# The 48 weight loads issued by GpSimd instead of SyncE

## The chip, the cores and the metric

One core of one Trainium2 chip runs one program. The metric is device time in microseconds (us) of one execution; lower is better. The profile comes from one further execution of the same program.

## The reference, cut to what matters

The inputs q, k, v are 4 x 8 x 576 x 64 in float32, omega is 128 x 64 and the weights of two feed-forward blocks are **float64** in memory. Three parts follow each other:

```python
phi(x):  h = x*scale @ omega.T - sum((x*scale)**2)/2;  h -= max(h, last axis);  exp(h)/sqrt(128)
kv = einsum('bhsm,bhsd->bhmd', phi(k), v);  z = sum(phi(k), axis=2)
x  = (phi(q) @ kv) / (phi(q) . z + 1e-6)           # then to [2304, 512]
h  = x @ w_in;  y = max(0.01*h, h) @ w_out         # w_in 512x2048, w_out 2048x512
h  = y @ w2_in; s = h*softmax(h); s = layernorm(s)*g_ln;  out = s @ w2_out   # 512x1024, 1024x512
```

## The kernel before, in words

The tokens are cut into 18 tiles of 128. For each tile there is a k unit and a q unit (load, squares, scale, transpose, projection on TensorE, maximum on VectorE, exp on ScalarE); the k units add up kv on TensorE, the q units draw x from it. The first block runs over pairs of tiles j = 0 to 8: stage 1 (`st1`, h = x @ w_in, L1087 for j = 0 in float32, L1093 for the rest as three float16 products), its evacuation (L1109 to L1111), stage 2 (`st2`, L1133 for j = 0, L1137 for the rest). The second block (`mlp2_in`, L1255 and L1373; `mlp2_out`, L1578) follows.

**The weights.** All four matrices come in 48 pieces of 128 rows by 512 float64 values, so 128 x 4096 bytes or 512 KB each: 16 of w_in and 16 of w_out early in the run (loads 0 to 31 in order of issue), 8 of w2_in and 8 of w2_out late (loads 32 to 47). `piece` (L363) does one. It takes one of four staging buffers `wraw`, starts the load (L374), and has the float64 bits turned into float32: either ScalarE reads the buffer (L388) or GpSimd does (L393, after which VectorE joins the sign, L396), and in both cases VectorE reads it last (L399) and the buffer is free. So load n + 4 cannot start before the L399 of load n has ended.

**What sets the order.** A planner in the program (`Issue`) plays all work through once, with durations written into the code, and writes every instruction down at the moment it is planned. Each engine then runs its own instructions strictly in that written order, each one waiting for its semaphores. Loads, stores and DMA transposes are planned on one queue, "DMA", and written into SyncE's stream: 113 copies and 119 transposes. An engine that issues a DMA waits for what the DMA needs (a free buffer, say) at its place in the stream, and what is written behind waits with it. GpSimd issues no DMA before the change; it computes some squares (L675), the first step of 26 weight pieces (L393), high parts of features (L876) and two steps of some weight cuts (L338, L340).

TensorE too has a fixed order. Up to 300 small products with zeros (L488, `warm_up`) are planned into places where it has nothing else; they are instructions like the others and take their time.

**The written order around the loads.** Loads and GpSimd's own instructions follow each other so: loads 0, 1, 2; L675 of the first k tile pair; L393 of load 0; load 3; L393 of load 1; loads 4 to 11; L675 of the first q pair; load 12; L393 of load 11; load 13; L393 of load 12; loads 14 to 20; L393 of load 18; load 21; L393 of load 21; loads 22, 23, 24; L393 of load 23; load 25; two L876; L338 and L340; load 26; L876; load 27; L876; L338; load 28; L340; L393 of load 28; loads 29, 30, 31; the last two L393 of this group. Late in the run: loads 32, 33, 34; L393 of load 32; load 35; L393 of loads 33, 34, 35; load 36; its L393; loads 37, 38; L393 of load 37; load 39; and so on in turn.

In SyncE's own order the load of the first k pair (L244, raw<-in_k_dram) and the two of omega (L499) stand among loads 0 to 3, and the first big transpose T<-hl (L705) stands between loads 21 and 22.

Of the kernel before, what the change touches and what calls it, by code (L numbers as in the profile page):

```python
# [27 lines left out]
class Issue:  # L28
# [13 lines left out]
    SP = {"DMA": (0.42, 2.3), "DT": (1.27, 1.65)}  # L42
# [121 lines left out]
def either(key, n, a, b):  # L164

    return a() if n in X[key] else b()
# [14 lines left out]
def linear_attention_moe_kernel(  # L181
# [14 lines left out]
    V, A, G, PE, SP = nc.vector, nc.scalar, nc.gpsimd, nc.tensor, nc.sync  # L196
# [74 lines left out]
    def mk(pool, tag, shape, dt):  # L271
        return pool.tile(shape, dt, name=tag, tag=tag, bufs=BUFS[tag])
# [90 lines left out]
    def piece(src, r0, c0, n, x, pool, nr):  # L363

        yield "get", "wraw"
        u = h = None
        if src.dtype == F32:
            yield "op", "DMA", 1.58, lambda: SP.dma_start(out=x, in_=src[r0:r0 + 128, c0:c0 + n])
        else:
            h = {}  # L370

            def load():
                h["r"] = mk(pool, "wraw", [128, n, 2], I32)
                SP.dma_start(out=h["r"].rearrange("p n w -> p (n w)"),  # L374
                             in_=src[r0:r0 + 128, c0:c0 + n].bitcast(I32))
            yield "op", "DMA", 1.58, load

            hw = lambda: h["r"][:, :, 1].bitcast(F32)  # L380
            xi = x.bitcast(I32)

            def shift():
                yield "op", "V2", 0.38, lambda: V.tensor_scalar(out=xi, in0=xi, scalar1=3, scalar2=None,
                                                               op0=ALU.logical_shift_left)

            def sign_A():
                yield "op", "A", 0.63, lambda: A.activation(out=x, in_=hw(), func=AF.Prelu, scale=2.0 ** -112,  # L388
                                                            alpha=-2.0 ** 32)
                yield from shift()  # L390

            def sign_V():
                yield "op", "G", 0.75, lambda: G.tensor_scalar(out=x, in0=hw(), scalar1=2.0 ** -112, scalar2=1.0,  # L393
                                                               op0=ALU.mult, op1=ALU.mult)
                yield from shift()
                yield "op", "V2", 0.62, lambda: V.scalar_tensor_tensor(  # L396
                    out=xi, in0=h["r"][:, :, 1], scalar=-(1 << 31), in1=xi, op0=ALU.bitwise_and, op1=ALU.bitwise_or)
            yield from either("ya", nr, sign_A, sign_V)
            yield "op", "V2", 0.62, lambda: V.scalar_tensor_tensor(  # L399
                out=xi, in0=h["r"][:, :, 0], scalar=29, in1=xi, op0=ALU.logical_shift_right, op1=ALU.bitwise_or)  # L400
        yield "put", "wraw"
# [1282 lines left out]
```

## Time and profile before

| | |
|---|---|
| time, median of 3 runs | 702.56 us (702.26, 702.56, 704.22) |
| the profiled execution, its time and its span | 701.82 us, 700.0 us |
| mean granted TensorE clock in it | 0.996 of full speed |
| busy share of the span: TensorE, VectorE, ScalarE, GpSimd | 98%, 70%, 59%, 20% |
| DMA queue of SyncE | 183536 packets, 80.37 MB, 49.8% of 16 engines' span |
| chain of work that ended last, largest shares | TensorE 74%, issue 7%, DMA 6%, ScalarE 6%, VectorE 4%, GpSimd 1% |

PE is TensorE, PEld its weight load, DVE VectorE, ACT ScalarE, POOL GpSimd, SP or SPq SyncE and its DMA queue. "Idle before, releaser" says how long the engine stood before an instruction and which work ended that; issuing a DMA does not count as busy. A time of a DMA "to landing" runs from its issue to the moment its semaphore shows all data there.

### The profile page before, as it was taken

The numbers are of one execution on the slowest core, as the hardware profiler recorded it, in microseconds if no ns is written. First come the engines' busy times: TensorE is split into PE (matmuls) and PEld (weight loads), VectorE is DVE, ScalarE is ACT, GpSimd is POOL, SyncE is SP. The second block draws the span as 40 slices with busy tenths as digits, with TensorE's granted clock in tenths as the row PEclk, the third lists the DMA queues.
The fourth block names the chain that finished last, engine by engine and source line by source line (L and its number), as shares of the span: only waits on it lengthen the run. The fifth ranks groups of instructions, "written<-read, shape, count | busy, mean of one in ns | idle before, by whom it ended". The sixth has DMA issues, their size and how long they took to land.

```text
span 700.0 us, 13443 instructions
## 1 busy us (share of the span) xinstructions
PE 684.4 (98%) x5120; PEld 453.4 (65%) x5120; DVE 486.6 (70%) x1211; ACT 416.1 (59%) x848; POOL 139.9 (20%) x174
## 2 busy tenths in 40 slices
PE   7989999999999999999999999999999999999997
PEld 7989885587766666767767666666654444444443
DVE  6988889699866567755965558953489897976410
ACT  4777987797766665656546535655244366756611
POOL 2010220433221110111101012534031111322210
PEclk9999999999999999999999999999999999999999
DMA  9895997696536442633725556501003323464541
GB/s 287 239 276 173 250 230 164 122 154 150 118 73 97 106 93 59 115 70 76 137 46 106 107 165 225 123 1 31 1 6 79 64 44 81 76 122 90 121 121 45
DMA packets 183600, 81.23 MB, mean 116 GB/s; under 512 B 146416, under 2 KB 175088, under 8 KB 183536
## 3 DMA queue, kind: packets, MB, share of 16 engines
q1 hardware_dynamic: 183536, 80.37, 49.8%
q8 instruction: 40, 0.66, 0.4%
q14 instruction: 24, 0.20, 0.1%
HBM read 41.75 MB, written 4.72 MB: 66 GB/s over the span
## 4 chain that ended last, share of the span: by engine, by line
PE 74%; issue 7%; DMA 6%; ACT 6%; DVE 4%; POOL 1%; SPq 1%; POOLq 0%; ACTq 0%; DVEq 0%
PE h L1093 18%; PE y L1137 16%; PE h L1578 13%; PE h L1373 6%; PE h L1087 3%; PE h L1255 3%; PE y L1373 3%; PE kv L853 2%; ACT qe L789 2%; PE y L1133 2%; DMA v<-in_v_dram 2%; PE a L1011 1%; DVE mx L774 1%; DMA raw<-in_k_dram 1%; DMA scr<-in_omega_dram 1%
## 5 line engine op out<-in xcount | busy, mean ns | idle before, releaser
L1137 PE MATMUL y<-w,g 128*128 128x512 f16 x768 | 176.0, 379 | 0.0
L1093 PEld LDWEIGHTS <-w 128*128 128x128 f16 x1536 | 148.2, 98 | 25.1 <-issue 1.1
L1137 PEld LDWEIGHTS <-g 128*128 128x128 f16 x768 | 73.9, 98 | 77.2 <-DVE g L1111 0.7
L1093 PE MATMUL h<-xy,w 128*128 128x256 f16 x960 | 111.9, 273 | 0.0
L1111 DVE TENSOR_TENSOR g<-h,g 128x512 f16<-128x512 f32 x64 | 44.0, 688 | 45.6 <-ACT g L1110 45.4
L1109 ACT ACTIVATE h<-h 128x512 f32<-128x512 f32 x64 | 38.1, 595 | 61.0 <-PE h L1093 60.6
L1093 PE MATMUL h<-xT,w 128*128 128x256 f16 x576 | 67.8, 273 | 0.1
L1578 PE MATMUL h<-wo,w 128*128 128x512 f16 x288 | 64.1, 379 | 0.0
L789 ACT ACTIVATE qe<-a,nb,sc 128x128 f32<-128x128 f32 x128 | 47.2, 468 | 15.6 <-DVE nb L780 13.8
L1578 PEld LDWEIGHTS <-w 128*128 128x128 f16 x288 | 28.2, 98 | 34.0
L774 DVE TENSOR_REDUCE mx<-a 128x4 f32<-128x512 f32 x63 | 41.5, 684 | 10.3 <-PE a L767 8.1
L876 POOL TENSOR_SCALAR qf<-qe 128x512 f16<-128x512 f32 x32 | 20.2, 634 | 110.5 <-ACT qe L789 84.6
L1110 ACT ACTIVATE g<-h 128x512 f16<-128x512 f32 x64 | 38.7, 604 | 1.2
L1588 ACT ACTIVATE osb<-h,c_out 128x512 f32<-128x512 f32 x18 | 12.3, 682 | 44.0 <-PE h L1578 41.1
L879 DVE SCALAR_TENSOR_TENSOR qf<-qe,qf 128x512 f16<-128x512 f32 x32 | 23.7, 740 | 16.1 <-POOL qf L876 16.1
L789 ACT ACTIVATE ke<-a,nb,sc 128x128 f32<-128x128 f32 x64 | 23.4, 469 | 16.6 <-DVE nb L780 15.0
L675 POOL TENSOR_TENSOR scr<-raw 128x1024 f32<-128x1024 f32 (+1 forms) x8 | 14.4, 1805 | 91.3 <-DMA raw<-in_q_dram 81.1
L1578 PE MATMUL h<-wo,lnT 128*128 128x512 f16 x144 | 32.2, 379 | 0.0
L1373 PE MATMUL h<-w 128*128 128x512 f16 x126 | 29.8, 379 | 0.7 <-ACT w L1431 0.7
L667 DVE TENSOR_REDUCE sq<-scr 128x16 f32<-128x1024 f32 (+1 forms) x20 | 22.1, 1107 | 11.5 <-POOL scr L675 7.6
L1373 PEld LDWEIGHTS <-w 128*128 128x128 f16 x168 | 16.4, 98 | 20.7 <-issue 1.0
L1087 PE MATMUL h<-xT,w 128*128 128x256 f32 x128 | 29.7, 383 | 0.0
(256 smaller groups left out, 1298.4 us busy)
## 6 DMA issues: line engine op xcount, KB each, us to landing
wraw<-in_moe_w_in_dram SPq DMA_DIRECT2D x24, 512.0 KB, 5.8
wraw<-in_moe_w_out_dram SPq DMA_DIRECT2D x24, 512.0 KB, 4.6
v<-in_v_dram SPq DMA_DIRECT2D x12, 512.0 KB, 4.4
raw<-in_k_dram SPq DMA_DIRECT2D x8, 512.0 KB, 4.2
raw<-in_q_dram SPq DMA_DIRECT2D x8, 512.0 KB, 4.8
out_dram<-osb SPq DMA_DIRECT2D x16, 256.0 KB, 2.3
v<-in_v_dram SPq DMA_DIRECT2D x6, 128.0 KB, 3.6
raw<-in_k_dram SPq DMA_DIRECT2D x4, 128.0 KB, 3.8
```

The costliest lines, as they stand in the source:

```text
L667: yield "op", "V", 0.07 + 0.54 * m, lambda: V.tensor_reduce(out=st["sq"], in_=tiles(st["scr"]), axis=AX.X, op=ALU.add)
L774: yield "op", "V", 0.6, lambda: V.tensor_reduce(out=u["mx"][:, hh::2], in_=w["ps"], axis=AX.X, op=ALU.max)
L789: A.activation(out=x[:, h, :], in_=w["ps"][:, h, :], func=AF.Exp, scale=st["sc"], bias=u["nb"][:, 2 * h + hh:2 * h + hh + 1])
L879: yield "op", "V" if stay else "V2", 0.62, lambda: V.scalar_tensor_tensor(out=w["f"][:, :, 1, :], in0=w["e"], scalar=2.0 ** 14, in1=w["f"] ...
L1087: PE.matmul(ps[:, f, :], lhsT=stash(w1, c * KC + kc)[:, o:o + 128], rhs=xT[j][:, kc, :], start=(kc == 0), stop=(kc == KC - 1))
L1093: PE.matmul(ps[:, f, :], lhsT=w1[:, c * KC + kc, w, o:o + 128], rhs=xT[j][:, :, xo + kc, :], start=(n == 0), stop=(n == 3 * KC - 1))
L1109: yield "op", "A", 0.48, lambda: A.activation(out=ps, in_=ps, func=AF.Prelu, scale=2.0 ** -19, alpha=0.01)
L1110: yield "op", "A", 0.48, lambda: A.activation(out=gg[:, 0], in_=ps, func=AF.Copy)
L1111: yield "op", "V", 0.6, lambda: V.tensor_tensor(out=gg[:, 1], in0=ps, in1=gg[:, 0], op=ALU.subtract)
L1137: PE.matmul(y_ps[j][t], lhsT=gg[:, a, f, ts], rhs=w2[:, 2 * p + f, w, :], start=(ends[0] and f == 0 and n == 0), stop=(ends[1] and f == 1 ...
L1373: PE.matmul(dst, lhsT=lhs(x, c), rhs=rhs(w, c), start=(fresh and n == c == 0), stop=(n == 2 and c == 1), skip_group_check=True)
L1578: PE.matmul(ps, lhsT=t[:, a, f, :], rhs=W["o"][:, f, w, :], start=(j == 0 and f == 0), stop=(j == 2 and f == KF2 - 1))
```

## The change: what it does

The engine that issues the load in `piece` is GpSimd (`G`) instead of SyncE (`SP`). The planner still plans the load on its "DMA" queue with the same duration, so the places in the written order stay as they are; only the stream into which the instruction goes is another one.

```diff
             def load():
                 h["r"] = mk(pool, "wraw", [128, n, 2], I32)
-                SP.dma_start(out=h["r"].rearrange("p n w -> p (n w)"),
+                G.dma_start(out=h["r"].rearrange("p n w -> p (n w)"),
                              in_=src[r0:r0 + 128, c0:c0 + n].bitcast(I32))
             yield "op", "DMA", 1.58, load
```

## Rows read from the trace of the kernel before

**Rows 1.** Stretches: window; us; PE, PEld, DVE, ACT, POOL busy (count); clock; DMA; GB/s.
```profile
0.00:20.00 20.00, 15.93 (x167) 14.94 (x167) 13.78 (x31) 9.69 (x19) 3.96 (x12) 1.00 0.93 298
...
40.00:60.00 20.00, 17.48 (x158) 16.71 (x155) 15.79 (x45) 14.13 (x34) 0.47 (x2) 0.91 0.87 251
60.00:80.00 20.00, 18.91 (x138) 17.31 (x137) 18.29 (x57) 17.28 (x42) 2.20 (x3) 1.00 0.70 210
80.00:100.00 20.00, 20.00 (x141) 17.46 (x140) 16.39 (x41) 16.85 (x36) 7.69 (x9) 1.00 0.93 213
...
400.00:450.00 50.00, 50.00 (x339) 33.06 (x338) 36.18 (x67) 25.09 (x54) 14.63 (x18) 1.00 0.61 176
```

**Rows 2.** Waits of TensorE: engine, line, releaser: us in total, times, longest.
```profile
PE kv L853 <- DMA v<-in_v_dram: 2.0, 2, 1.6
...
PE h L502 <- DMA scr<-in_omega_dram: 1.0, 1, 1.0
```

**Rows 3.** Waits of SyncE's own DMA queue, same columns.
```profile
SPq L374 <- DVE w L399: 33.1, 20, 5.0
```

**Rows 4.** Chain that ended last, in order of time: start us, us, what.
```profile
5.06 7.63 DMA scr<-in_omega_dram
...
68.47 7.50 DMA T<-hl
...
493.73 1.73 PE h L1255 x8
```

**Rows 5.** Timeline of TensorE: start us, us, engine, line, names, count.
```profile
7.66 4.14 PE L488 MATMUL kv<-nil 128*128 128x128 f16 x62
...
44.85 1.09 PE L735 MATMUL h<-ident,qe 128*128 128x128 f32 x8
```

**Rows 6.** Line 374: issue ns min/median/max, then landing us.
```profile
L374 SPq DMA_DIRECT2D wraw<-in_moe_w_in_dram x24: 327/386/1163, 1.2 to 421.4; - x24
...
DMA to landing us min/median/max: 3.4/5.4/8.6
```

**Rows 7.** GpSimd by line, 0 to 130 us: busy us, mean ns, idle before.
```profile
L340 POOL TENSOR_TENSOR w<-w 128x512 f16<-128x512 f32 x3 | 3.8, 1263 | 0.2
```

**Rows 8.** Timeline of ScalarE: start us, us, what, idle before and releaser.
```profile
9.28 0.69 ACT L388 ACTIVATE w<-wraw 128x512 f32<-128x512 f32 x1 [7.28 <-DMA wraw<-in_moe_w_in_dram]
...
16.91 0.68 ACT L388 ACTIVATE w<-wraw 128x512 f32<-128x512 f32 x1 [0.42 <-DMA wraw<-in_moe_w_in_dram]
...
42.24 0.67 ACT L388 ACTIVATE w<-wraw 128x512 f32<-128x512 f32 x1 [4.15 <-DMA wraw<-in_moe_w_out_dram]
42.82 1.13 ACT L789 ACTIVATE qe<-a,nb 128x128 f32<-128x128 f32 x4
```

**Rows 9.** Timeline of SyncE's DMA queue, same columns.
```profile
33.76 0.33 SPq L374 DMA_DIRECT2D wraw<-in_moe_w_in_dram  x1
34.36 0.33 SPq L374 DMA_DIRECT2D wraw<-in_moe_w_out_dram  x1
...
68.47 3.87 SPq L705 DMA_TRANSPOSE T<-hl  x1
72.45 1.46 SPq L374 DMA_DIRECT2D wraw<-in_moe_w_out_dram  x3
```

**Rows 10.** Timeline of GpSimd, same columns.
```profile
34.78 1.89 POOL L675 TENSOR_TENSOR scr<-raw 128x1024 f32<-128x1024 f32 x1 [26.32 <-DMA raw<-in_q_dram]
37.99 0.79 POOL L393 TENSOR_SCALAR w<-wraw 128x512 f32<-128x512 f32 x1 [1.31 <-DMA wraw<-in_moe_w_in_dram]
...
80.11 0.62 POOL L876 TENSOR_SCALAR qf<-qe 128x512 f16<-128x512 f32 x1 [0.45 <-ACT qe L789]
...
460.95 1.47 POOL L340 TENSOR_TENSOR wi<-wi 128x512 f16<-128x512 f32 x1
```

**Rows 11.** Timeline of VectorE, 69 to 73 us: the last readers of two buffers.
```profile
69.27 0.68 DVE L399 SCALAR_TENSOR_TENSOR w<-wraw,w 128x512 int32<-128x512 int32 x1
...
71.38 0.68 DVE L399 SCALAR_TENSOR_TENSOR w<-wraw,w 128x512 int32<-128x512 int32 x1
```

## The prediction

> **What bounds the kernel now.** I read the stretches first [rows 1]. TensorE is busy without a gap from 80 us on (20.00 of 20.00, and 50.00 of 50.00 between 400 and 450), so nothing that the loads gain there can shorten the run. Its idle time is at the front: 20 - 15.93 = 4.1 us in 0 to 20, 2.5 us in 40 to 60, 1.1 us in 60 to 80. DMA is crowded in just these stretches (shares of 0.93 and 0.87, about 300 GB/s). TensorE's own waits [rows 2] say what ends those gaps: 1.0 us for omega, 2.0 us for v. Beside them it runs a fixed filler, such as 62 products with zeros from 7.66 us for 4.14 us [rows 5], which no earlier load takes away. The chain of waits [rows 4] shows two DMAs on it that are slow for their size: omega's 32 KB needs 7.63 us, since it was issued behind three weight loads and more on the same queue, and T<-hl takes 7.50 us. Last I read the streams of ScalarE, SyncE and GpSimd [rows 8 to 10] and compared the written order with their times.
>
> So time can be won only out of some 3 us of DMA waits at the front; it is lost wherever an engine's fixed order makes TensorE wait for something later than today.
>
> **What the change removes.** SyncE issues 48 instructions fewer, 0.33 to 0.39 us each [rows 6], and no longer stands 33.1 us in 20 waits for a free staging buffer [rows 3]. I cost that at nothing: it was waiting with the load that came next in any case, its buffer's last reader L399 ended the wait, and what stands behind (raw, v, transposes) waits for readers of its own; if one of them was ready meanwhile, up to the longest such wait, 5.0 us, is a gain for that DMA, and TensorE's 3 us of DMA waits are all that can be won with it. The loads are bound by the four buffers, not by SyncE; only few can start sooner. The clear case is loads 22 to 24: their buffers come free at about 69.95, 71.4 and 72.06 (the first and the third are 69.27 + 0.68 and 71.38 + 0.68 [rows 11]), and SyncE issues them from 72.45 on, after T<-hl, whose issue alone takes 3.87 us [rows 9].
>
> **What it adds.** GpSimd must describe 48 transfers. The trace has no such instruction. Bounds: SyncE's 0.33 us [rows 6] from below, GpSimd's longest kind, L675 with 1.89 us [rows 10], from above. I take 1.26 us, the mean of L340 [rows 7], a whole GpSimd pass over 512 columns and near the middle. A description that costs less than nothing is excluded, since the engine must at least dispatch it. In throughput that is harmless: 48 x 1.26 = 60 us more on an engine that is idle 80% of the run. What counts is the order.
>
> **What moves, in order of time.**
>
> *A, start.* Loads 0 to 2 now run beside the first k load and omega instead of between them. A 512 KB load occupies the engines for 0.524 MB / 298 GB/s = 1.8 us [rows 1]. The first k load can be slowed by up to that, and I take half, 0.9; omega's wait of 1.0 us [rows 2] can go, for the zeros ahead of it in TensorE's order end at 7.66 + 4.14 = 11.80 [rows 5], 0.9 us before omega lands at 12.69 [rows 4]. Sum about 0; ends -1.0 and +0.8.
>
> *B, load 4.* ScalarE already waits 0.42 us for it at 16.91 [rows 8], and the next thing it does is on TensorE's path. GpSimd is free there, so the load is later by the description alone, 1.26 - 0.39 = 0.9 us at most; with some crowding gone I take +0.4; ends 0 and +0.9.
>
> *C, load 13.* This is the place where the order bites. On SyncE it went out at 34.36 [rows 9]. On GpSimd it stands behind L675, which waits for the first q pair until 34.78 and ends at 36.67, then behind load 12, then behind L393 of load 11, which ends at 37.99 + 0.79 = 38.78 [rows 10]. So it starts 4.4 us later and takes 1.26 us to describe: 40.04. From the end of issue to landing a load takes 3.4 - 0.4 = 3.0 us at least and 5.4 - 0.4 = 5.0 us in the median [rows 6]: it lands at 43.0 to 45.0. Today ScalarE stands 4.15 us before L388 of this very load, until 42.24, and the exp of the first q tile is next in its order at 42.82 [rows 8]; TensorE transposes that exp's result at 44.85 [rows 5]. So TensorE gets it 0.8 to 2.8 us later. I take the middle, +1.8. TensorE's waits for v of 2.0 us [rows 2] may shrink, but they would only become a wait at 44.85. If L675 and load 11 come sooner, nothing is lost: ends -2.0 (the v waits gone, load 13 in time) and +2.8.
>
> *E, T<-hl.* TensorE turns to this transpose's result as soon as it is there, at 68.47 + 7.50 = 75.97 [rows 4]. Loads 22 to 24 stood behind it; now load 22 can be described from 69.95, and its data flow some 3 us later, beside the last 3 us of T. At a third of the engines for the weights T loses +1.0; ends 0 (T was limited by its own issue, 3.87 us) and 5.3 (three loads of 1.8 us pass it whole).
>
> *F, 80 to 130 us.* Load 25 now stands ahead of L876, which ran at 80.11 [rows 10]; with a description of 1.26 us, and no longer a wait for its buffer than the one that SyncE had, L876 is 1.3 us later, and VectorE and a transpose wait for it. TensorE's gapless work hides it [rows 1]: 0, up to +1.3.
>
> *G, the late loads.* Load 35 goes from before the L393 of load 32 to behind it, so behind that load's landing, and the next ones follow. VectorE, 72% busy (36.18 of 50), will stand a few us. TensorE's f16 work is the cover, without a gap there [rows 1], and the last piece of w2_in is cut at 460.95 + 1.47 = 462.42 [rows 10], 31 us ahead of its first use at 493.73 [rows 4]: 0, up to +2 if an evacuation is caught behind a waiting VectorE.
>
> Sum: 0 + 0.4 + 1.8 + 1.0 + 0 + 0 = **+3.2 us** on the profiled 701.82, so 705.0. That execution lies 0.74 below the median of 702.56, with 1.8 us outside its span that the change leaves alone; on the median it is **705.8 us**.
>
> **The rivals.** *R1, relief, not slower.* The loads leave SyncE's queue, so omega and v no longer sit behind them: 1.0 + 2.0 us of TensorE's waits go [rows 2]. The point that decides is load 13: if it lands by 42.2, C's loss is nothing. For it: omega's 7.63 us and a crowded queue. Against it: L675 waits for a q load on GpSimd itself. Time 702.6 - 3.0 = 699.6.
>
> *R2, nothing.* The same 16 DMA engines, four buffers, a TensorE order that hides the rest; C and the relief cancel. Time 702.6. Against it: two gaps would have to match by chance.
>
> *R3, the weights overtake.* With the loads on a queue of their own the engines serve both queues in turn, and what SyncE issues first no longer goes first. Then A is +0.8, B +0.9, C +2.8 and E +5.3: +9.8, so 712.4. For it: T and the loads collide fully in the written order. Against it: T's long issue time says that it is not limited by the engines alone. The Trainium skill, "DMA: Bandwidth & Descriptors", section "Queues, rings and completion order", has each engine go round its queues by the packet; by that rule the 4 KB pieces of a weight load would take more than their share beside smaller ones, which would make R3's price. No row of before has two busy queues, so the trace neither agrees nor disagrees.
>
> *R4, dear descriptions.* If a description takes 1.89 us or more, the first three take 5.7 us and load 2 lands 8.7 to 10.7 us after GpSimd is ready, against ScalarE's wait for it until 9.28 [rows 8]. I price A at +1.5, B at 1.89 - 0.39 = +1.5, C at 2.8 + 0.6 = +3.4, E at +2, F at +1.9 and G at +2: +12.3, so 714.9. Against it: each load is only 128 rows of 4 KB. The Trainium skill, "SBUF — State Buffer", section "Who interferes with whom", speaks against the change here: GpSimd's descriptor writing is blocked while VectorE holds the shared port pair in one of its two-port modes, and a DMA issued from SyncE is not. The trace before cannot show it; by that rule R4 would hold wherever VectorE is 80% busy and more, as in 40 to 80 us.
>
> **How the numbers follow.** Chances: the forecast 0.33, R1 0.20, R2 0.27, R3 0.12, R4 0.08. Within 0.3% means within 2.1 us, about what a measurement of this kernel can tell from no change: 700.5 to 704.7. Faster is R1, 0.20. Same is R2, 0.27. Slower is the forecast, R3 and R4, 0.53. The range goes from R1's 699.6, rounded to 699.5, to 713, a little above R3; it leaves out a third of R1 and most of R4, some 0.15 together. The forecast's own range is 704.7 to 708.5.
>
> **What would show each step.** On SyncE no L374 is left; a second DMA queue carries 25 MB. The issue of a load on GpSimd shows the price of a description: near 1.3 us, or R4. C: ScalarE's L388 that ended its wait at 42.24 now waits till 43 or later with a longer wait, and TensorE's idle time in 40 to 60 grows from 2.5 us by about 2; if it shrinks, R1 is at work. B: the wait of 0.42 at 16.91 grows. A: TensorE's wait for omega is gone. E: T lands later than 7.5 us after its issue, and TensorE waits for it at 76. F and G: TensorE stays gapless from 80 us on; if it has new gaps there, I mis-sized the cover. The prediction is wrong if TensorE passes 80 us earlier than now, or if the loss stands in the late stages.

## The result: 0.9% slower, and all of it is lost before 90 us

| | before | changed |
|---|---|---|
| time, median of 8 runs each | 702.53 us (701.54 to 705.30) | 709.37 us (706.05 to 711.13) |
| ratio, 95% interval | | 1.0091 (1.0071 to 1.0110) |
| the profiled execution, its time and its span | 701.82 us, 700.0 us | 711.01 us, 709.2 us |
| mean granted TensorE clock in it | 0.996 | 0.991 |

The forecast was 705.8, so 3.2 us of loss where 6.8 were measured; the time also lies above the forecast's own range of 704.7 to 708.5. One of the 12 executions of run e8_only_v below took 797.0 us at a granted clock of 0.848, and its ratio leaves that one out. What is called the first profile below is that of this run. The stretches of the changed kernel, with the columns of [rows 1]:

```profile
0.00:20.00 20.00, 15.64 (x153) 14.84 (x153) 11.44 (x23) 7.50 (x12) 8.60 (x20) 1.00 0.82 255
20.00:40.00 20.00, 17.35 (x151) 16.78 (x152) 16.42 (x49) 12.83 (x42) 2.75 (x5) 0.91 0.68 202
40.00:60.00 20.00, 15.99 (x150) 14.67 (x149) 13.60 (x33) 11.52 (x32) 5.92 (x8) 0.91 0.81 236
60.00:80.00 20.00, 19.36 (x151) 18.58 (x151) 16.07 (x57) 15.73 (x40) 4.67 (x7) 0.91 0.63 184
80.00:100.00 20.00, 18.54 (x119) 16.10 (x118) 15.19 (x34) 17.07 (x37) 7.61 (x11) 1.00 0.87 222
...
400.00:450.00 50.00, 50.00 (x378) 35.15 (x377) 33.97 (x75) 25.17 (x57) 17.91 (x27) 1.00 0.66 181
```

Beside [rows 1]: TensorE has new idle time in 20 to 40 (2.65 us against 0.44) and 40 to 60 (4.0 against 2.5), the granted clock is 0.91 in three stretches where it was in one, and DMA moves less in each of the first four (255 against 298 GB/s in the first). The late stage is as full as before. The same TensorE instruction, found in both traces, tells where the time goes: L735 is 2.0 us late at 20.4, 4.8 at 30.4 and 6.4 at 42.2 (the first q tile); L735 of qe is 6.7 us late at 51.6; the first product after T<-hl is 9.6 us late at 85.6, and from there on the shift hardly changes (9.2 at the end).

TensorE's waits, columns as in [rows 2]:

```profile
PE h L735 <- ACT qe L789: 1.9, 1, 1.9
PE kv L853 <- ACT ke L789: 1.7, 1, 1.7
PE h L502 <- DMA scr<-in_omega_dram: 1.6, 1, 1.6
PE a L766 <- DMA T<-hl: 1.5, 1, 1.5
...
PE h L735 <- DMA raw<-in_q_dram: 1.2, 1, 1.2
...
PE kv L853 <- DMA v<-in_v_dram: 0.6, 1, 0.6
```

Of the 2.0 us for v in [rows 2], 1.4 are gone; omega's wait grew from 1.0 to 1.6, and four waits are new. Line 374 (issue ns, first and last start) answers to [rows 6]:

```profile
L374 POOL DMA_DIRECT2D wraw<-in_moe_w_in_dram x24: 530/540/767, 1.5 to 431.0; - x24
L374 POOL DMA_DIRECT2D wraw<-in_moe_w_out_dram x24: 530/578/763, 15.3 to 457.7; - x24
```

So GpSimd needs 0.53 to 0.77 us to issue a load, not the 1.26 that I took. And this is the page's list of DMA queues (packets, MB, share of 16 engines); q0 is new:

```profile
q1 hardware_dynamic: 176624, 55.20, 38.1%
q0 software_dynamic: 6912, 25.17, 10.8%
```

### The profile page after: what moved, and what is told of

It is laid out like the page before. It is cut to its first block, busy times and chain, and to the rows that moved or that the text cites. A ratio compares the mean times of both kernels' runs of the same rounds, so it can differ in the third digit from the quotient of the medians.

```text
span 709.2 us, 13460 instructions
## 1 busy us (share of the span) xinstructions
PE 688.9 (97%) x5120; PEld 457.2 (64%) x5120; DVE 488.2 (69%) x1211; ACT 416.1 (59%) x848; POOL 168.4 (24%) x222
## 4 chain that ended last, share of the span: by engine, by line
PE 73%; issue 8%; DMA 7%; ACT 6%; DVE 5%; POOL 1%; SPq 0%; POOLq 0%; ACTq 0%; DVEq 0%
PE h L1093 17%; PE y L1137 16%; PE h L1578 13%; PE h L1373 6%; PE h L1087 3%; DMA v<-in_v_dram 3%; PE h L1255 3%; PE y L1373 3%; ACT qe L789 2%; PE kv L853 2%; PE y L1133 2%; DVE mx L774 2%; PE a L1011 1%; DMA T<-hl 1%; ACT ke L789 1%
## 5 line engine op out<-in xcount | busy, mean ns | idle before, releaser
L789 ACT ACTIVATE qe<-a,nb,sc 128x128 f32<-128x128 f32 x128 | 47.2, 469 | 16.8 <-DVE nb L780 13.8
L876 POOL TENSOR_SCALAR qf<-qe 128x512 f16<-128x512 f32 x32 | 20.3, 636 | 110.0 <-ACT qe L789 84.2
L789 ACT ACTIVATE ke<-a,nb,sc 128x128 f32<-128x128 f32 x64 | 23.4, 469 | 16.6 <-DVE nb L780 15.0
L675 POOL TENSOR_TENSOR scr<-raw 128x1024 f32<-128x1024 f32 (+1 forms) x8 | 14.6, 1828 | 63.4 <-DMA raw<-in_q_dram 55.8
```

The lines of the kernel that those rows point to most:

```text
L789: A.activation(out=x[:, h, :], in_=w["ps"][:, h, :], func=AF.Exp, scale=st["sc"], bias=u["nb"][:, 2 * h + hh:2 * h + hh + 1])
```

## Where the first 3 us go

Two chains lead from the loads to TensorE at the start. Chain 1: load 1, its L393 on GpSimd, VectorE's steps for loads 0 to 2 in their fixed order (L384, L396, L399), then L505 (omT), then TensorE's L763. Chain 2: v, its copy L573 on ScalarE and what stands behind that there (among it the exp L789 to ke), then TensorE's L853; and the second v load, which waits for the buffer. In the timeline of the kernel before (start, us; an instruction that waited for a DMA starts when it lands):

```profile
7.81 0.65 POOL L393 TENSOR_SCALAR w<-wraw 128x512 f32<-128x512 f32 x1 [0.17 <-DMA wraw<-in_moe_w_in_dram]
...
11.16 1.06 ACT L573 ACTIVATE scr<-v 128x1024 f16<-128x1024 f32 x1 [1.19 <-DMA v<-in_v_dram]
...
13.16 0.61 DVE L505 TENSOR_SCALAR omT<-h 64x128 f32<-64x128 f32 x2
...
13.50 1.16 PE L763 MATMUL a<-omT,T 128*128 128x128 f32 x8
...
14.50 1.06 PE L763 MATMUL y<-omT,T 128*128 128x128 f32 x8
```

The same instructions where all 48 loads are on GpSimd, from the profile of run c_after, which was timed beside its parts below:

```profile
10.15 0.66 POOL L393 TENSOR_SCALAR w<-wraw 128x512 f32<-128x512 f32 x1 [2.10 <-DMA wraw<-in_moe_w_in_dram]
...
13.04 1.06 ACT L573 ACTIVATE scr<-v 128x1024 f16<-128x1024 f32 x1 [0.74 <-DMA v<-in_v_dram]
...
14.65 0.60 DVE L505 TENSOR_SCALAR omT<-h 64x128 f32<-64x128 f32 x2
...
14.98 1.44 PE L763 MATMUL a<-omT,T 128*128 128x128 f32 x8 [0.78 <-DVE omT L505]
...
16.21 1.92 PE L763 MATMUL y<-omT,T 128*128 128x128 f32 x8
```

Load 1 is 2.3 us late, omT and L763 1.5 us. Then the clock adds as much again: eight products take 1.92 us instead of 1.06, near the ratio of 2.4 to 1.2 GHz, after TensorE has stood for 1.55 us before L502 and 0.78 us before L763 (1.02 and none in the kernel before). The four groups of L763 last 5.47 us here and 3.84 before. So L735 behind them is 3.1 us late, half by waiting and half by the clock.

In the first profile two waits end almost together: omega, landing at 14.32 instead of 12.69, holds L502 until 14.45, and VectorE's last L399 before omT ends at 14.80. L763 starts at 15.13, 1.6 us late, and its products run at full speed there, although TensorE had stood for 1.64 us before L502. So a stand is not always followed by a lower clock.

Why is load 1 late? Before, one queue served in order of issue: k 5.05, load 0 6.42, load 1 7.74, first half of omega 7.93, load 2 9.26, v 11.07, load 3 12.43, second half of omega 12.69 (landings from the trace). In c_after two queues share: k 5.08, omega's first half 5.25, load 0 7.32, load 1 10.08, load 2 11.60, v 12.95, load 3 13.09, omega's second half 13.31. The same bytes end 0.6 us later (1.6 in the first profile), but what was wanted first is 0.9 to 2.3 us late. v went out 1.4 us **earlier** (1.86 against 3.29) and lands 1.9 us later; the weights overtake v, and v slows the weights. The queues in 2 to 13 us of the changed kernel, columns as above:

```profile
q0 software_dynamic: 576, 2.10, 51.7%
q1 hardware_dynamic: 2865, 1.38, 44.6%
```

They share the engines' time almost evenly, and GpSimd's 4 KB packets carry 60% of the bytes in it. The Trainium skill, "DMA: Bandwidth & Descriptors", section "Queues, rings and completion order", lets an engine go round its queues by the packet, in a sense of packet that takes in several descriptors. The trace bears out that both queues are served in turn; in the packets that the profile counts it is 1 to 5, not 1 to 1.

## The experiments

All have the computing instructions of the kernel before, in its order on every engine; only who issues a DMA differs. `number` counts the 48 loads in order of issue, from 0. Run c_after is the changed kernel again, to compare on one chip:

```diff
-                G.dma_start(out=h["r"].rearrange("p n w -> p (n w)"),
+                (G if next(number) >= 0 else SP).dma_start(out=h["r"].rearrange("p n w -> p (n w)"),
```

> All 48 loads on GpSimd, the changed kernel itself, timed beside its parts on one chip. Both theories: some 6.5 us above before (ratio 1.009), with a mean granted clock of 0.991 against 0.995; the clock alone is worth 0.004 x 700 = 2.8 us of it, if a run's time goes with its clock as in the runs of before (0.70 us per 0.001).

Measured: 708.38 us against 701.40, ratio 1.0107 (1.0071 to 1.0144). The granted clock of its 6 runs has a median of 0.9925, before 0.995. A straight line through each kernel's own runs (time against granted clock) reads, at an equal clock of 0.994, 706.9 us for c_after and 702.2 for before. So 4.7 of the 7.0 us are there at an equal clock, and the rest goes with it, at before's 0.52 to 0.70 us per 0.001. This is a split by a fit over 6 and 23 runs, not by an edit.

**Which loads?** Four runs put only some of them on GpSimd, the others on SyncE.

```diff
-                G.dma_start(out=h["r"].rearrange("p n w -> p (n w)"),
+                (G if next(number) <= 11 else SP).dma_start(out=h["r"].rearrange("p n w -> p (n w)"),  # e5_only_0_11
+                (G if next(number) in range(12, 18) else SP).dma_start(out=h["r"].rearrange("p n w -> p (n w)"),  # e6_only_12_17
+                (G if next(number) in range(18, 32) else SP).dma_start(out=h["r"].rearrange("p n w -> p (n w)"),  # e7_only_18_31
+                (G if next(number) >= 32 else SP).dma_start(out=h["r"].rearrange("p n w -> p (n w)"),  # e4_only_late
```

> Only loads 0 to 11 go out from GpSimd. Theory (the loss starts at the front: weights on their own queue delay omega, v and raw q): L853 is reached at 23 us instead of 20.1, L735 of raw q at 40 or later instead of 35.7, and 3.5 to 6.5 us of the loss are here: ratio 1.005 to 1.009. Rival (what counts is load 13 behind L675 and T beside loads 22 to 24): ratio 1.000 to 1.003.

Measured: 706.36 us, ratio 1.0090 (1.0054 to 1.0125). The theory held: L735 is again 3.1 us late at 20.3, and L735 of raw q starts at 39.87 instead of 35.74. That is just short of the 40 expected, and L853 came at 22.62 instead of 23. Twelve loads make most of the whole loss.

> Only loads 12 to 17 go out from GpSimd, with the front as before. Theory (step C): load 13 is described only behind L675 and lands late; ScalarE's wait before its L388 is 5 to 6 us instead of 4.15, TensorE's L735 of qe is 1 to 2.8 us late, ratio 1.0015 to 1.004. Rival (with raw q in time L675 ends in time, and the v wait that goes pays for the rest): ratio 0.998 to 1.001.

Measured: 702.82 us, ratio 1.0020 (1.0004 to 1.0036), inside the theory's range, though the interval reaches the rival's 1.001 too. Its timeline is the clean view of step C:

```profile
37.06 0.61 POOL L374 DMA_DIRECT2D wraw<-in_moe_w_out_dram  x1
...
41.53 2.00 PE L853 MATMUL kv<-v,ke 64*128 64x65 f32 x16
...
44.04 0.66 ACT L388 ACTIVATE w<-wraw 128x512 f32<-128x512 f32 x1 [5.82 <-DMA wraw<-in_moe_w_out_dram]
44.60 1.12 ACT L789 ACTIVATE qe<-a,nb 128x128 f32<-128x128 f32 x4
45.59 1.16 ACT L789 ACTIVATE qe<-y,nb 128x128 f32<-128x128 f32 x4
...
45.00 2.28 PE L735 MATMUL h<-ident,qe 128*128 128x128 f32 x8 [1.48 <-ACT qe L789]
...
47.08 1.92 PE L763 MATMUL a<-omT,T 128*128 128x128 f32 x8
```

Load 13 is described behind L675, and ScalarE gets it at 44.04, 1.8 us after 42.24 [rows 8]. TensorE's L735 starts only 0.15 us late (45.00 against 44.85 [rows 5]): v, out of the line behind loads 12 and 13, came earlier, L853 ran 1.4 us sooner than its 42.92, and its wait moved behind it. But L735 then takes 2.28 us where [rows 5] has 1.09. Its eight transposes need the results of ScalarE's eight exps, which end only at 46.75; in the kernel before they ended at 44.98:

```profile
43.82 1.16 ACT L789 ACTIVATE qe<-y,nb 128x128 f32<-128x128 f32 x4
...
45.78 1.06 PE L763 MATMUL a<-omT,T 128*128 128x128 f32 x8
```

So the L763 behind L735 starts at 47.08 instead of 45.78. These 1.3 us are what load 13 costs TensorE here. This L763 takes 1.92 us where it was 1.06, at a granted clock of 0.66 in 45 to 50, and three groups later TensorE is 2.6 us late. That the moved wait brought the lower clock is not shown: in run e4 below, where nothing before 400 us is moved and the wait stands before L853 as it did in the kernel before, the clock in 45 to 50 is 0.66 as well:

```profile
44.61 1.42 PE L735 MATMUL h<-ident,qe 128*128 128x128 f32 x8
45.81 1.92 PE L763 MATMUL a<-omT,T 128*128 128x128 f32 x8
```

> Only loads 18 to 31 go out from GpSimd. Theory (step E): T<-hl lands 1.4 us later and L766 waits for it, ratio 1.002; step F costs nothing. If parts add up, this and the two other parts give the whole of +6.5 us. Rival (with everything before it in time T is not slowed, and only the whole gives the late T): ratio 0.999 to 1.001.

Measured: 703.63 us, ratio 1.0032 (1.0008 to 1.0056), nearer the theory than the rival, though the interval reaches both. T lands 8.06 us after its issue (7.50 before; 1.4 us more were expected), and this wait of TensorE is there:

```profile
PE a L766 <- DMA T<-hl: 0.7, 1, 0.7
```

The rest of this trace's lateness is not step E: TensorE is 3.2 us late at 50.80 already, before the first of the moved loads goes out at 55.07, with a granted clock of 0.76 in 40 to 60.

The parts sum to 0.9 + 0.2 + 0.3 + 0.1 = 1.5% against 1.07%. One late part can hide the next: in c_after, where the front is late, TensorE does not wait at L735 of qe at all. But the intervals are too wide to show that the parts do not simply add up.

> Only loads 32 to 47 (400 us and later) go out from GpSimd, the first 32 from SyncE. Theory (step G: TensorE's gapless work hides what the late loads change): 702.5 +- 1, same as before, without a gap of TensorE from 400 us on. Rival (the late loads have a share in the loss): 704 or more, with idle time of TensorE in 400 to 520 us.

Measured: 702.48 us, ratio 1.0008 (0.9990 to 1.0025). Step G costs nothing that shows, and TensorE has no gap there:

```profile
400.00:450.00 50.00, 50.00 (x338) 32.88 (x337) 34.29 (x66) 23.90 (x52) 22.56 (x32) 1.00 0.61 174
450.00:500.00 50.00, 50.00 (x346) 33.52 (x344) 27.71 (x47) 25.01 (x48) 18.64 (x21) 1.00 0.09 23
```

**What comes back?** Four runs leave all on GpSimd but some. The expected times of the first three were made from a before of 702.53 us; on their chip it took 701.73, so ratios are the better comparison.

```diff
-                G.dma_start(out=h["r"].rearrange("p n w -> p (n w)"),
+                (SP if next(number) in (0, 1, 2, 3) else G).dma_start(out=h["r"].rearrange("p n w -> p (n w)"),  # e1_start_sync
+                (SP if next(number) == 13 else G).dma_start(out=h["r"].rearrange("p n w -> p (n w)"),  # e2_load13_sync
+                (SP if next(number) in (22, 23, 24) else G).dma_start(out=h["r"].rearrange("p n w -> p (n w)"),  # e3_t_sync
+                (SP if next(number) in (0, 1, 2, 3, 13, 22, 23, 24) else G).dma_start(out=h["r"].rearrange("p n w -> p (n w)"),  # e11_eight_sync
```

> Loads 0 to 3 go out from SyncE again, the other 44 from GpSimd. Theory (the early loads on a queue of their own go round by round with what SyncE issues, so that omega and v land later, and the slower start pulls TensorE's clock down): L502 is reached at 12.8 instead of 14.45, L853 at 20.1 instead of 23.3 us, the granted clock in 20 to 40 us goes back towards 1.00, and some 3.2 to 4.8 us of the 6.8 come back: 704.6 to 706.2. Rival (the loss comes from what stands in order on GpSimd behind L675, not from the queue): the first four loads wait for nothing there, so it stays at 709.4 +- 1, and load 13 is as late as in the changed kernel.

Measured: 706.28 us against 701.73, ratio 1.0075 (1.0047 to 1.0103): between the theory's range (as ratios 1.003 to 1.005) and the rival's (1.008 to 1.011), with an interval that reaches both, and 2 us better than c_after by the middle, with overlapping intervals. The trace is clearer: L763 is at 13.68 (13.50 before), L853 at 19.69, even 0.4 us sooner than before, and the granted clock in 20 to 40 is 1.00. The start is mended. But TensorE falls behind again 20 us later, by load 13 behind L675 (L735 1.1 us late, and L763 behind it, at 48.06, 2.3):

```profile
45.98 2.28 PE L735 MATMUL h<-ident,qe 128*128 128x128 f32 x8 [1.93 <-ACT qe L789]
```

> Load 13 alone goes out from SyncE again. Theory (step C: on GpSimd it stands behind L675, which waits for raw q): ScalarE's wait of 6.03 us before L388 shrinks to 2 or less, TensorE's L735 of qe comes 1.9 us earlier against the instructions ahead of it, and since TensorE then has a shorter gap at 50 us its clock may not fall: 1.9 to 3.8 us come back, 705.6 to 707.5. Rival (the load is late because the start is late, or because the DMA engines are crowded): 709.4 +- 0.7.

Measured: 706.34 us, ratio 1.0080 (1.0046 to 1.0114). ScalarE's wait before that L388 is 1.75 us instead of 6.03, as the theory had it, and TensorE does not wait there, as it did not in c_after either; its front is late as in c_after. In time the gain of some 2 us is again within the intervals, and the ratio lies between the theory's 1.004 to 1.007 and the rival's 1.009 to 1.011.

> Loads 22 to 24 go out from SyncE again, so behind T<-hl as before. Theory (step E: they run beside T on the other queue): T lands 7.5 instead of 8.86 us after its issue, the wait of 1.5 us at L766 goes, 708.0. Rival (T is limited by itself and only starts later): T's wait stays, 709.4 +- 0.5.

Measured: 706.86 us, ratio 1.0076 (1.0046 to 1.0106). T lands in 7.23 us, and TensorE does not wait for it. But T took 7.70 us in c_after too, where TensorE waited only 0.3 us for it, so part of the 1.5 us in the first profile was chance, and what this edit won in time is not settled. That the loads slow T is shown by all traces together: T takes 7.66 to 8.86 us in the six where loads 22 to 24 go out beside it, and 7.06 to 7.68 in the eight where SyncE issues them behind it, 8.04 against 7.27 on the mean.

> Loads 0 to 3, 13 and 22 to 24 from SyncE, the other 40 from GpSimd: the three edits that alone gave ratios of 1.0075, 1.008 and 1.0076 against 1.0107. Theory (each takes a part of its own away, some 2 us each): ratio 1.000 to 1.004. Rival (one gap takes the place of another, so that the parts don't add up: loads 4 to 11 beside v, raw q and the transposes of omega still come out of order): ratio 1.005 to 1.008.

Measured: 703.96 us against 702.06, ratio 1.0024 (1.0003 to 1.0045): the theory. Eight loads of 48 bring back 0.8 of 1.07%; singly they brought 0.32, 0.27 and 0.31, which adds up to 0.9. With intervals of 0.2 to 0.4% on each ratio, from three chips, this is in line with parts that add up, and no proof of it.

**Queue or engine?** Two runs move the first v load, which stood between loads 2 and 3.

```diff
+    vq = iter([G])
...
-            SP.dma_start(out=dst[:, :, o:o + 2 * D], in_=src[b, :, 0:S4, :].rearrange(
+            (next(vq, SP) if src is v else SP).dma_start(out=dst[:, :, o:o + 2 * D], in_=src[b, :, 0:S4, :].rearrange(
...
-                G.dma_start(out=h["r"].rearrange("p n w -> p (n w)"),
+                (SP if next(number) >= 0 else G).dma_start(out=h["r"].rearrange("p n w -> p (n w)"),  # e8_only_v
+                (G if next(number) >= 0 else SP).dma_start(out=h["r"].rearrange("p n w -> p (n w)"),  # e9_v_too
```

> All 48 weight loads go out from SyncE as before; only the first load of v (L244, 512 KB, issued at 3.29 between loads 2 and 3) goes out from GpSimd, before its L675. Theory (what costs is that a second queue breaks the order of issue: v runs beside loads 0 to 2 whichever of the two is on GpSimd): loads 1 and 2 land at about 10.0 and 11.4 instead of 7.7 and 9.3, TensorE's L763 begins at 15.0 instead of 13.5 and runs slow for a part, +2.5 to +3.5 us at L735, ratio 1.003 to 1.005. Rival (the loss comes with weight loads being issued by GpSimd): loads 1 and 2 land as before, ratio 0.999 to 1.001.

Measured: 702.39 us against 702.06, ratio 1.0012 (0.9989 to 1.0035). The theory fell as it was put: v beside the weights does not by itself cost time. Its timeline says why:

```profile
8.53 0.65 POOL L393 TENSOR_SCALAR w<-wraw 128x512 f32<-128x512 f32 x1 [0.91 <-DMA wraw<-in_moe_w_in_dram]
...
11.41 0.68 ACT L388 ACTIVATE w<-wraw 128x512 f32<-128x512 f32 x1 [9.40 <-DMA wraw<-in_moe_w_in_dram]
...
13.81 1.16 PE L763 MATMUL a<-omT,T 128*128 128x128 f32 x8
...
20.07 1.97 PE L853 MATMUL kv<-v,ke 128*128 128x65 f32 x16
```

Load 2 is late by the 2.1 us expected (11.41 against 9.28 [rows 8]), but load 1 by only 0.7, and v lands earlier (10.08 against 11.07). VectorE's order has room for the one (L763 is 0.3 us late), and the other helps ScalarE. Lateness of some transfer is no loss; in these first 20 us only that of load 1, of v and of omega has shown as one.

> All 48 loads go out from GpSimd as in the changed kernel, and the first load of v with them, at its old place between loads 2 and 3. Theory: the big transfers of the start stand in one queue again, loads 1 and 2 land at 7.5 to 8.2 and 9.0 to 9.7, omega (alone behind k on SyncE) lands by 6, L763 begins at 13.5 or earlier and +3.1 us of the loss at L735 go; ratio 1.005 to 1.007 instead of 1.0107. Rival (GpSimd's queue itself is slower or is described too late): loads 1 and 2 land past 10, ratio 1.009 or more.

Measured: 709.68 us, ratio 1.0115 (1.0084 to 1.0147), so the rival's ratio and not better than c_after in time. The start went nearly as the theory said, though later at each point: load 1 landed at 8.46 (expected 7.5 to 8.2), load 2 at 10.80 (9.0 to 9.7), omega at 6.40 (by 6), and L763 began at 13.59, 0.1 us late. So 0.7 us of load 1's lateness is there even with v behind it in its own queue, but it costs TensorE next to nothing. What takes the place is chain 2:

```profile
12.77 1.06 ACT L573 ACTIVATE scr<-v 128x1024 f16<-128x1024 f32 x1 [1.28 <-DMA v<-in_v_dram]
...
13.59 1.16 PE L763 MATMUL a<-omT,T 128*128 128x128 f32 x8 [0.35 <-DVE omT L505]
...
21.83 1.97 PE L853 MATMUL kv<-v,ke 128*128 128x65 f32 x16 [1.56 <-DMA v<-in_v_dram]
```

The first v is 1.6 us late, behind the loads in GpSimd's queue and beside SyncE's; its buffer comes free late, the second v load goes out at 13.95 instead of 12.51 and now shares with loads 4 to 6; TensorE waits for it, and its L763 behind that takes 5.42 us instead of 3.79. So both chains have to be in time, and mending one leaves the loss to the other.

**Can a second queue help?** The loads stay on SyncE; the two loads of omega go out from ScalarE.

```diff
-            yield "op", "DMA", 0.2, lambda c=c: SP.dma_start(out=om2[:, c], in_=omega)
+            yield "op", "DMA", 0.2, lambda c=c: A.dma_start(out=om2[:, c], in_=omega)
```

> All 48 loads from SyncE; only the two loads of omega (32 KB each) go out from ScalarE, which has nothing to do then. Theory (a second queue is a way past the line): omega lands by 6 instead of 12.7, L502 comes at 12.0 instead of 12.8, the loads lose 0.3 us at most, ratio 0.998 to 1.000, so up to 1.0 us faster than before. Rival (two queues cost the big transfers more than their bytes): loads 0 to 2 land over 1 us later, ratio above 1.002.

Measured: 701.78 us against 702.06, ratio 0.9993 (0.9975 to 1.0010). Omega is there at 5.33 instead of 12.69, and TensorE's wait for it is gone; but omT on VectorE stands behind L399 of load 2, so L763 starts 0.07 us earlier, and no more:

```profile
12.20 0.28 PE L502 MATMUL h<-ident,scr 128*128 128x128 f32 x1
...
13.43 1.16 PE L763 MATMUL a<-omT,T 128*128 128x128 f32 x8 [0.51 <-DVE omT L505]
```

None of the runs beats the kernel before by more than can be measured. No run issued the weight loads from a third engine: that any second queue would cost as much as GpSimd's is not shown.

## Why the prediction was right in sign and range, and short in size

*A, start (0, ends -1.0 and +0.8): the step that failed.* I reckoned with the k load and omega alone. The price is in load 1 and v, which I did not follow to L505 and L853, and in omega, which came later and not sooner (its wait grew from 1.0 to 1.6 us where the sign that I set for A was that it goes): +2.0 us at 20 us in the first profile and +3.1 in c_after and e5, +4.8 and more by 30 us. What happened is R3's mechanism ("the engines serve both queues in turn"), which I had given 0.12; R3's own A of +0.8 was as small. The relief of 1.0 us for omega that I allowed here, and R1 with it, was none: e10 took that wait away and won 0.07 us.

*B, load 4 (+0.4).* It landed 1.5 us late (18.39 against 16.88), but ScalarE was late itself and did not wait for it: it has no price of its own.

*C, load 13 (+1.8).* Right for ScalarE, by luck, and too large for TensorE. The written order that I worked from was off by a place here: load 12 stands before L675, and load 13 right behind it, ahead of the L393 of load 11 (load 3 likewise stands before the first L675, and load 25 between the two L876). With a description of 0.6 instead of 1.26 us the start was 37.06 in e6, not 40. Yet ScalarE got load 13 at 44.04, +1.8 to the digit, since from the end of its issue to landing it took 6.3 us, longer than the 3.0 to 5.0 that I took: two errors that cancel. And I put ScalarE's lateness down to TensorE whole. At 44.85 TensorE had not been waiting for the exps but came from L853, which had waited for v, so there was some slack: in e6 the products behind L735 are 1.3 us late. In the changed kernel:

```profile
42.13 1.90 POOL L675 TENSOR_TENSOR scr<-raw 128x1024 f32<-128x1024 f32 x1 [2.52 <-DMA raw<-in_q_dram]
...
43.98 0.60 POOL L374 DMA_DIRECT2D wraw<-in_moe_w_out_dram  x1
...
50.61 0.66 ACT L388 ACTIVATE w<-wraw 128x512 f32<-128x512 f32 x1 [6.03 <-DMA wraw<-in_moe_w_out_dram]
...
51.58 2.28 PE L735 MATMUL h<-ident,qe 128*128 128x128 f32 x8 [1.87 <-ACT qe L789]
```

The gain at v that I set against it came too (1.4 us).

*E, T<-hl (+1.0).* T landed 8.86 us after its issue in the first profile (+1.36, and 1.5 us of waiting), 7.70 in c_after. On the mean of all traces the loads cost T 0.8 us: the term was about right, though TensorE's wait for it went from 1.5 us down to 0.3.

*F and G (0).* Right: the first profile's shift does not grow after T, and e4 costs nothing.

*R4, dear descriptions.* Wrong: 0.77 us at the most. The Trainium skill, "SBUF — State Buffer", section "Who interferes with whom", warned of descriptors held up behind VectorE in its two-port modes; with VectorE busy 80% of 20 to 40 and of 60 to 80 us, no issue took over 0.77 us, so no such hold-up shows in this trace, which does not tell VectorE's modes.

*The sum.* No term was there for the clock. By the fit above, 2 to 3 of the 7 us go with it. The traces tie falls of the clock to the early loads: in 0 to 40 us the granted clock is 1.00 in all eight traces in which SyncE issues loads 0 to 3 (before, e1, e4, e6, e7, e8, e10, e11), and 0.91 to 0.98 in all six in which GpSimd does (the first profile, c_after, e2, e3, e5, e9). In 40 to 60 us no load is seen behind them: the clock is below 1.00 in every trace, 0.91 in before and 0.83 in e4, which differ in nothing until 400 us. R2 was excluded by the interval. Two readings were loose, without weight in the sum: the 300 GB/s hold for 0 to 20 us, not for 40 to 60 (251 [rows 1]), and VectorE is 79% busy in 40 to 60, not 80% and more.

## What to carry to other kernels

A second DMA queue does not only relieve the first: here it replaced the order in which transfers were issued by sharing, so that what was first in line ended near the others. Before moving transfers to another queue, list what lands first now and follow each one's readers through the fixed orders of all engines; a wait on the busiest engine is often only the last of several that end at almost the same time, as omega's was. And a late start of TensorE can cost twice, as in c_after's first 20 us: read the granted clock and the time of the same product behind it. But before blaming the clock, see whether a slow group only waits for its operands one by one, as L735 did in e6, and whether a kernel without the edit has the same slow stretch, as e4 had.

## What was not expected of the hardware

GpSimd issued a load of 128 rows of 4 KB in 0.53 to 0.77 us, against SyncE's 0.33 us at the least [rows 6]; the v load, in pieces of 512 bytes, took it 0.93 and 1.10 us. Two queues that were both full had 51.7% and 44.6% of the DMA engines' time. Runs of the changed kernel scatter more (706.05 to 711.13 us over 8) than those of before (701.54 to 705.30), and the longer ones mostly have the lower granted clock (0.994 at 706.05, 0.989 at 711.13, though 0.987 at 710.64).
